# Pooled attention feeding a four-expert MoE: two-bank attention, a first batch pooled by matmuls, and fixed slots for batch 1

## The chip, the cores and the metric

The kernel runs on one core of a Trainium2 chip. The metric is device time in microseconds (us) of one execution. "Before" takes 545.05 us, the median of its first 3 runs (544.22 to 545.55).

Engines, as the profile names them: PE is the matmul engine, PEld its weight loads, DVE the vector engine, ACT the scalar engine, POOL the engine that issues the loads, SP the engine that issues the stores and DMA transposes. Times in the text are us from the start of the span unless something else is said. The span of a profile is about 2 us shorter than the device time of the same run.

## The reference

```python
# shortened: the softmax is written out in the reference, and out starts as zeros
def _attn_ref(q, k, v):                      # B=8, H=8, S=576, D=64
    k_p = k.reshape(B, H, S // 8, 8, D).mean(axis=3)      # pool 8 keys into 1: 72 keys
    v_p = v.reshape(B, H, S // 8, 8, D).mean(axis=3)
    scores = q @ k_p.transpose(0, 1, 3, 2) / sqrt(D)
    attn = softmax(scores)
    return attn @ v_p

def _moe_ref(x, domain_probs, w1, w2):       # x: 4608 x 512, E=4, F=1024
    p = domain_probs / (domain_probs.sum(-1, keepdims=True) + 1e-09)
    for e in range(E):
        out += p[:, e:e + 1] * (np.maximum(x @ w1[e], 0) @ w2[e])
```

Every token goes through all four experts, so nearly all the arithmetic is the MoE: two matmul layers, four times.

## The kernel before

The tokens are taken in nine chunks of 512 (eight batches, then the 8 x 64 left-over tokens). A *step* is one chunk through one expert. While PE works on the experts of chunk b, the attention of batch b+1 is done in small *pieces* between its matmuls.

The up-projection is a seven-product scheme (`up_seven`) in two halves j. Each half has four *slots*, `between(0)` to `between(3)`. In a slot PE does a share of the `down` matmuls of the step before, and the next attention piece is issued. DVE takes its instructions in the order issued (a trace below shows it). The code that the argument needs, with cuts marked:

```python
    def fold(raw, hs):                                    # DVE: 8 rows -> 4 -> 2
        nc.vector.tensor_add(out=raw[:, hs, 0:4, :], in0=raw[:, hs, 0:4, :], in1=raw[:, hs, 4:8, :])
        nc.vector.tensor_add(out=raw[:, hs, 0:2, :], in0=raw[:, hs, 0:2, :], in1=raw[:, hs, 2:4, :])

    def fold_keys(b, hs):                                 # 2 -> 1, written twice
        raw = raws[("kraw", b)]
        fold(raw, hs)
        for dup in range(2):
            nc.vector.tensor_add(out=kps[b % 2][0:SP, hs, dup, :], in0=raw[:, hs, 0, :], in1=raw[:, hs, 1, :])
    # ... fold_values: the same, written once
    # ... attention(b), for b >= 2, is a list of pieces, one popped whenever `due` reaches 1:
        add(opening)             # DMA transpose of q; fold_keys over all 8 heads; loads of b+1
        add(folded_values)       # fold_values over all 8 heads
        for _ in range(3):
            add(lambda: None)    # an empty piece: a pause
        for pair in range(NPAIR):
            add(lambda pair=pair: scores(b, pair))
            add(lambda pair=pair: exps(b, pair, 1))
    # ... then 4 x (context, context, turn), 3 pauses, combine_x

    def up_seven(c, e, j, between):
        # ...
        g, d, s = bank(), bank(), bank()                  # three PSUM banks
        product(c, e, j, 1, g, True)
        r1 = keep(g)                                      # ACT copies the bank to SBUF
        between(0)
        product(c, e, j, 2, s, True)
        relu_sum(top[:, :, 0:TH], s, r1)                  # DVE, relu-sum #1
        product(c, e, j, 6, g, False)
        r2 = keep(g)
        between(1)
        product(c, e, j, 5, d, True)
        product(c, e, j, 7, g, False)
        r3 = keep(g)
        relu_sum(low[:, :, TH:NT], d, r3)                 # DVE, relu-sum #2
        between(2)
        product(c, e, j, 4, g, False)
        nc.scalar.activation(out=low[:, :, 0:TH], in_=g[:], func=ACT.Relu)
        between(3)
        product(c, e, j, 3, d, False)
        relu_sum(top[:, :, TH:NT], d, r2)                 # DVE, relu-sum #3

    def down(c, e, j, n):                                 # slot n of half j
        first = (0, 3, 7, 12, 16)                         # 3, 4, 5, 4 matmuls
        for at in range(first[n], first[n + 1]):
            r, fc = 2 * j + at // FCH, at % FCH
            # ... one 128x512 matmul into sums[r]
            if fc == FCH - 1:                             # at = 7 and 15: slots 2 and 3
                merge(c, e, r, sums[r])                   # DVE; ACT for expert 0

    # ... the loads, in issue order:
        load_k(0); load_q(0); load_v(0); load_w1(0); load_probs(); load_w1(1)
        load_w2(0); load_w1(2); load_w2(1); load_w1(3)
        attention_first(); norm_probs(); combine_x(0)
        load_k(1); load_q(1); load_v(1); load_w2(2); load_w2(3)   # ...
```

Some words for what follows. A *fold* adds rows of k or v pairwise on DVE, until one row stands for eight. PSUM is the memory, in banks, into which PE writes its results. A *relu-sum* adds such a bank to the copy that ACT kept of another one, and sets negative values to 0. *Forms* are the sums and differences of weight blocks, or of blocks of x, that the seven products multiply.

The softmax here doesn't subtract the row's maximum and nothing guards it: scores larger than these inputs give would overflow.

Of the kernel before, what the change touches and what calls it, by code (L numbers as in the profile page):

```python
# [18 lines left out]
def kernel(  # L19
# [25 lines left out]
    SPP = 80  # L45
    BIG = 3.0e38
# [15 lines left out]
    psum_a = ctx.enter_context(tc.tile_pool(name="psum_a", bufs=3, space=bass.MemoryType.PSUM))  # L62
    psum_h = ctx.enter_context(tc.tile_pool(name="psum_h", bufs=3, space=bass.MemoryType.PSUM))
    psum_o = ctx.enter_context(tc.tile_pool(name="psum_o", bufs=2, space=bass.MemoryType.PSUM))
# [11 lines left out]
    def groups(b):  # L76

        n = 2 if b == 0 else 1
        return [slice(i * H // n, (i + 1) * H // n) for i in range(n)]

    def load_kv(b, src, nm):
        raw = rawpool.tile([SP, H, POOL, D], BF16, name=nm)
        for hs in groups(b):
            nc.gpsimd.dma_start(
                out=raw[:, hs], in_=src[b, hs].rearrange("h (j r) d -> j h r d", r=POOL)
            )
        raws[(nm, b)] = raw

    def load_q(b):
        q_sb = qpool.tile([P, H, NR, D], BF16, name="q_sb")  # L90
        for hs in groups(b):
            nc.gpsimd.dma_start(  # L92
                out=q_sb[:, hs].rearrange("p h r d -> p h (r d)"),
                in_=q[b, hs, 0:NT, :].rearrange("h (p r) d -> p h (r d)", r=NR),
            )
        raws[("q", b)] = q_sb

# [57 lines left out]

    def fold(raw, hs):
        nc.vector.tensor_add(out=raw[:, hs, 0:4, :], in0=raw[:, hs, 0:4, :],  # L157
                             in1=raw[:, hs, 4:8, :])
        nc.vector.tensor_add(out=raw[:, hs, 0:2, :], in0=raw[:, hs, 0:2, :],  # L159
                             in1=raw[:, hs, 2:4, :])  # L160

    def by_dma(b):
        return b >= 2
# [8 lines left out]
    def keys(b, hs):  # L172
        if hs.start == 0:
            state[("kpT", b)] = apool.tile([P, H, SPP], BF16, name="kpT", bufs=3)
        if by_dma(b):
            nc.sync.dma_start_transpose(
                out=state[("kpT", b)][:], in_=kps[b % 2][:].rearrange("j h u d -> j (h u d)")
            )
            return
        kpt_ps = psum_a.tile([P, H, SP], BF16, tag="a", name="kpt_ps")  # L180
        for h in range(hs.start, hs.stop):
            nc.tensor.transpose(kpt_ps[:, h, :], kps[b % 2][0:SP, h], ident[:SP, :SP])  # L182
        nc.vector.tensor_copy(out=state[("kpT", b)][:, hs, 0:SP], in_=kpt_ps[:, hs])
# [8 lines left out]
    def queries(b, pair):  # L192
        q_sb = raws[("q", b)]
        if pair == 0:
            state[("qT", b)] = apool.tile([P, H, 2, P], BF16, name="qT", bufs=1)
        if by_dma(b):
            nc.sync.dma_start_transpose(
                out=state[("qT", b)][:].rearrange("c h r p -> c (h r) p"),
                in_=q_sb[:].rearrange("p h r d -> p (h r d)"),
            )  # L200
            return
        pool, tag = (psum_o, "o_ps") if b == 0 else (psum_a, "a")
        qt_ps = pool.tile([P, 2, 2, P], BF16, tag=tag, name="qt_ps")
        for hh in range(2):
            for rr in range(2):
                nc.tensor.transpose(
                    qt_ps[:, hh, rr, :], q_sb[:, 2 * pair + hh, 2 * rr:2 * rr + 2, :], ident[:]
                )
        copy = nc.scalar.copy if b == 0 and pair % 2 else nc.vector.tensor_copy
        copy(out=state[("qT", b)][:, 2 * pair:2 * pair + 2], in_=qt_ps[:])  # L210

    def scores(b, pair):
        kpT, qT = state[("kpT", b)], state[("qT", b)]
        if pair == 0:
            state[("expT", b)] = apool.tile([SP, H, 2, 2, P], BF16, name="expT", bufs=1)
        both = [psum_a.tile([P, 2, 2, P], F32, tag="a", name="sc_ps") for _ in range(2)]
        for hh in range(2):
            h = 2 * pair + hh
            for r2 in range(2):
                lo = r2 * D  # L220
                nc.tensor.matmul(  # L221
                    both[r2][0:SP, hh], lhsT=kpT[lo:lo + D, h, 0:SP], rhs=qT[lo:lo + D, h]
                )
        state[("sc", b, pair)] = both
        exps(b, pair, 0)

    def exps(b, pair, r2):
        nc.scalar.activation(  # L228
            out=state[("expT", b)][:, 2 * pair:2 * pair + 2, :, r2, :],
            in_=state[("sc", b, pair)][r2][0:SP], func=ACT.Exp, scale=EXP_SCALE,  # L230
        )

    def divide(c_ps, x_tok, half):
        inv = npool.tile([P, NPAIR], F32, name="inv")
# [6 lines left out]
    def context(b, r, half):  # L241
        expT, vp = state[("expT", b)], vps[b % 3]
        if ("x", b, r) not in state:
            state[("x", b, r)] = npool.tile([P, 2, NPAIR, D], BF16, name="x_tok", bufs=5)
        pool, tag = (psum_h, "h_ps") if b == 0 and half else (psum_a, "a")
        c_ps = pool.tile([P, NPAIR, D + 1], F32, tag=tag, name="c_ps")
        for i in range(NPAIR):
            h = half * NPAIR + i
            nc.tensor.matmul(  # L249
                c_ps[:, i, :], lhsT=expT[:, h, r // 2, r % 2, :], rhs=vp[:, h, :]  # L250
            )
        divide(c_ps, state[("x", b, r)], half)

    def flip(x_tok, dst, on_dma, copy=nc.vector.tensor_copy):
        flat = x_tok[:].rearrange("p a h d -> p (a h d)")
        if on_dma:
            nc.sync.dma_start_transpose(out=dst, in_=flat)
            return
        xt_ps = psum_a.tile([P, NPAIR, P], BF16, tag="a", name="xt_ps")
        for kc in range(KC):  # L260
            nc.tensor.transpose(xt_ps[:, kc, :], flat[:, kc * P:(kc + 1) * P], ident[:])  # L261
        copy(out=dst, in_=xt_ps[:])

    def turn(b, r):
        if r == 0:
            state[("xT", b)] = xpool.tile([P, KC, NT], BF16, name="xT")
        flip(state.pop(("x", b, r)), state[("xT", b)][:, :, r * P:(r + 1) * P], by_dma(b),
             nc.scalar.copy if b == 0 else nc.vector.tensor_copy)

    def rem_queries(i):  # L270
        q_rem = q_rems.pop(i)
        qTr = apool.tile([P, NPAIR, 2, REM], BF16, name="qTr")
# [6 lines left out]
    def rem_scores(i):  # L279
        qTr = state.pop(("qTr", i))  # L280
        both = [psum_a.tile([P, 2, NPAIR, REM], F32, tag="a", name="scr_ps") for _ in range(2)]
        for bb in range(2):
            kpT = state[("kpT", 2 * i + bb)]
            for pair in range(NPAIR):
                for hh in range(2):
                    lo = hh * D
                    nc.tensor.matmul(
                        both[hh][0:SP, bb, pair, :], lhsT=kpT[lo:lo + D, 2 * pair + hh, 0:SP],
                        rhs=qTr[lo:lo + D, pair, bb, :],
                    )  # L290
        expTr = apool.tile([SP, 2, 2, NPAIR, REM], BF16, name="expTr")
        for hh in range(2):
            nc.scalar.activation(out=expTr[:, hh], in_=both[hh][0:SP],
                                 func=ACT.Exp, scale=EXP_SCALE)
        state[("expTr", i)] = expTr

    def rem_context(i):
        expTr = state.pop(("expTr", i))
        x_tok = npool.tile([P, 2, NPAIR, D], BF16, name="x_tok", bufs=5)
        for half in range(2):  # L300
            c_ps = psum_a.tile([P, NPAIR, D + 1], F32, tag="a", name="c_ps")
            for j in range(NPAIR):
                h = half * NPAIR + j
                for bb in range(2):
                    nc.tensor.matmul(
                        c_ps[bb * REM:(bb + 1) * REM, j, :],
                        lhsT=expTr[:, h % 2, bb, h // 2, :], rhs=vps[(2 * i + bb) % 3][:, h, :],
                    )
            divide(c_ps, x_tok, half)
        state[("xr", i)] = x_tok  # L310

    def rem_turn(i):
        flip(state.pop(("xr", i)), x_rem[:, :, i * P:(i + 1) * P], True)

    def attention_first():

        lo, hi = groups(0)
        fold_keys(0, lo)
        keys(0, lo)
        fold_keys(0, hi)  # L320
        keys(0, hi)
        for pair in range(NPAIR):
            queries(0, pair)
            if pair:
                scores(0, pair - 1)
                exps(0, pair - 1, 1)
        scores(0, NPAIR - 1)
        exps(0, NPAIR - 1, 1)
        for half, hs in enumerate((lo, hi)):
            fold_values(0, hs)  # L330
            for r in range(NR):
                context(0, r, half)
                if half and r:
                    turn(0, r - 1)
        turn(0, NR - 1)

    def attention(b):

        every = slice(0, H)
# [4 lines left out]
        def opening():  # L344
            if by_dma(b):
                queries(b, 0)
            fold_keys(b, every)
            if by_dma(b):
                keys(b, every)
                load_next()  # L350

        def load_next():
# [5 lines left out]
        def folded_values():  # L358
            fold_values(b, every)
# [3 lines left out]
        def queried(pair):  # L363
            queries(b, pair)
            if pair == NPAIR - 1:
                load_next()

        add(opening)
        add(folded_values)
        if by_dma(b):  # L370
            for _ in range(3):
                add(lambda: None)
        else:
            add(lambda: keys(b, every))
            add(lambda: queried(0))
        for pair in range(NPAIR):
            if not by_dma(b) and pair + 1 < NPAIR:
                add(lambda pair=pair: queried(pair + 1))
            add(lambda pair=pair: scores(b, pair))
            add(lambda pair=pair: exps(b, pair, 1))  # L380
        for r in range(NR):
            add(lambda r=r: context(b, r, 0))
# [254 lines left out]
```

## Time and profile before

| reading | before |
|---|---|
| device time | 545.05 us |
| span of the profile | 543.2 us |
| first expert's first matmul | 25.22 |
| first expert done | 33.85 |
| PE's wait for the folded keys of batch 1 | 3.68 us, up to 54.30 |
| batch 1's first expert starts | 87.43 |
| PE's waits on relu-sums after that | 4.1 us, 6 times |

(87.43 is the fifth matmul of a row of eight in PE's timeline: its start, 87.00, and four steps of 0.109 us.)

From the page of before: the busy line (busy us, share of the span, instructions), then rows that cut the span into 40 slices of 13.6 us. The digits are tenths of a slice; the last row is GB/s moved.

```profile
PE 511.9 (94%) x3736; PEld 328.7 (61%) x3736; DVE 322.4 (59%) x599; ACT 233.5 (43%) x403; POOL 45.7 (8%) x64
...
PE   2696999999999999999999999999999999999996
...
GB/s 122 197 206 200 196 109 1 136 133 31 93 152 38 19 21 111 153 28 70 121 90 23 28 51 165 65 69 32 59 17 25 35 53 1 11 40 39 2 1 77
```

PE is short of full in slices 1, 2 and 4, all before 55 us, and in the last one. In slices 2 and 4 the loads run at about 200 GB/s. From slice 5 to the last but one PE's row is 9s, which leaves two things to gain: the start, and any single waits that a slice of 13.6 us does not show. A word of caution on the 94%: the Trainium skill ("Trainium Kernel Development and Optimization", section "Best Practices") says not to judge the distance to the roofline by matmul busy time. This trace agrees: records of 128x256 matmuls are 273 ns long, but four of them take 0.60 us, so they start 0.109 us apart and the records overlap.

The waits view of before, of PE alone (what was waited for: us in total, times, longest us):

```profile
PE kpt_ps L182 <- DVE kp L169: 14.4, 3, 7.8
PE g_ps L432 <- DVE H_sb L470: 4.1, 6, 0.8
PE c_ps L249 <- DVE vp L188: 2.5, 1, 2.5
```

The first line is the wait for folded keys: 7.8 and 2.9 us of it in the first attention, 3.68 in batch 1's. The second is the wait on relu-sums.

The windows view of before (start:end, length, busy us and count of PE, PEld, DVE, ACT, POOL, then the granted PE clock, the DMA share and GB/s):

```profile
50.00:60.00 10.00, 5.97 (x32) 3.32 (x30) 6.26 (x10) 0.97 (x2) 0.54 (x1) 0.66 1.30 201
...
88.00:540.00 452.00, 445.40 (x3261) 287.63 (x3258) 268.59 (x479) 199.04 (x344) 16.27 (x20) 1.00 0.32 59
```

After the wait at 50.6 to 54.3 the clock is down to 0.66 for those ten microseconds; in the long stretch after 88 it is full.

The timeline of before, PE's rows (start, us, engine, line, operation, count, and in brackets the idle time before it and what ended it):

```profile
25.22 8.79 PE L450 MATMUL h_ps<-xT,w_bf 128*128 128x512 bf16 x32 [0.67 <-ACT xT L262]
33.85 0.60 PE L432 MATMUL g_ps<-xT,w_bf 128*128 128x256 bf16 x4
...
54.30 0.66 PE L182 MATMUL kpt_ps<-ident,kp 72*128 72x72 bf16 x8 [3.68 <-DVE kp L169]
...
106.27 1.03 PE L432 MATMUL g_ps<-xf,w_bf 128*128 128x256 bf16 x8 [0.81 <-DVE H_sb L470]
```

And DVE's rows around that last wait:

```profile
98.67 1.21 DVE L157 TENSOR_TENSOR kraw<-kraw 72x2048 bf16<-72x2048 bf16 x1
...
101.31 0.68 DVE L470 CUSTOM_DVE_ANT_0 H_sb<-g_ps,r 128x512 bf16<-128x512 f32 x1
101.91 0.74 DVE L515 SCALAR_TENSOR_TENSOR acc<-o_ps,p_all,acc 128x512 f32<-128x512 f32 x1
102.57 1.21 DVE L157 TENSOR_TENSOR vraw<-vraw 72x2048 bf16<-72x2048 bf16 x1
...
104.88 0.74 DVE L515 SCALAR_TENSOR_TENSOR acc<-o_ps,p_all,acc 128x512 f32<-128x512 f32 x1
105.54 1.27 DVE L470 CUSTOM_DVE_ANT_0 H_sb<-g_ps,r 128x512 bf16<-128x512 f32 x2
```

The whole key fold (98.67 to 101.31) stands in slot 1, ahead of relu-sum #2. The whole value fold stands in slot 2. Relu-sum #3 comes at 105.54, and PE waits for it 0.81 us, because the next half's product 5 goes into the bank that it reads. The batch after this one waits once too (0.55 us).

### The profile page before, as it was taken

Reading aid. Unit: us, or ns where it says so; the run is one execution under the profiler, and the core shown is the slowest. Engines: PE = TensorE matmul, PEld = TensorE weight load, DVE = VectorE, ACT = ScalarE, POOL = GpSimd, SP = SyncE. Lnnn points to the kernel's source line nnn. Section 1 sums busy time; section 2 is a strip of 40 time slices with the busy share of each in tenths; the row PEclk is TensorE's granted clock in tenths of the full one; section 3 lists DMA queues with packets and bytes.
Section 4 is the critical chain, followed back from the end, with each engine's and each line's share of the span. In section 5 each row is a group of like instructions: output and inputs, shape, how many; then the busy total and the mean of one; then the engine's idle time right before and its main releaser. Section 6 shows DMA issues by size and latency. Waiting matters only on the chain.

```text
span 543.2 us, 9149 instructions
## 1 busy us (share of the span) xinstructions
PE 511.9 (94%) x3736; PEld 328.7 (61%) x3736; DVE 322.4 (59%) x599; ACT 233.5 (43%) x403; POOL 45.7 (8%) x64
## 2 busy tenths in 40 slices
PE   2696999999999999999999999999999999999996
PEld 1354556566656666566666665666566666666663
DVE  3725588837773767367836665568456644554453
ACT  1463343473346333643373345533653345334430
POOL 6632100200110000201100002000000000000000
PEclk9999899999999999999999999999999999999999
DMA  8999980681781014914831119331101010011003
GB/s 122 197 206 200 196 109 1 136 133 31 93 152 38 19 21 111 153 28 70 121 90 23 28 51 165 65 69 32 59 17 25 35 53 1 11 40 39 2 1 77
DMA packets 72954, 40.98 MB, mean 75 GB/s; under 512 B 42688, under 2 KB 68288, under 8 KB 72912
## 3 DMA queue, kind: packets, MB, share of 16 engines
q0 software_dynamic: 33744, 22.63, 29.2%
q1 hardware_dynamic: 39168, 17.77, 14.0%
q8 instruction: 29, 0.48, 0.4%
q14 instruction: 13, 0.11, 0.1%
HBM read 45.16 MB, written 9.44 MB: 101 GB/s over the span
## 4 chain that ended last, share of the span: by engine, by line
PE 84%; DVE 9%; DMA 5%; issue 1%; ACT 0%; POOL 0%; POOLq 0%; DVEq 0%
PE o_ps L501 41%; PE g_ps L432 36%; DMA vraw<-in_v_dram 4%; PE sc_ps L221 2%; DVE H_sb L470 2%; DVE acc L515 2%; PE h_ps L450 2%; PE c_ps L249 1%; DMA kraw<-in_k_dram 1%; DVE vraw L157 1%; DVE kraw L157 1%; DVE vraw L159 1%; PE xt_ps L261 1%; DVE kp L169 1%; DVE x_tok L236 0%
## 5 line engine op out<-in xcount | busy, mean ns | idle before, releaser
L501 PE MATMUL o_ps<-w_bf,H_sb 128*128 128x512 bf16 x1152 | 295.6, 380 | 0.0
L470 DVE CUSTOM_DVE_ANT_0 H_sb<-g_ps,r 128x512 bf16<-128x512 f32 x210 | 143.8, 687 | 162.6 <-ACT r L466 90.3
L432 PEld LDWEIGHTS <-w_bf 128*128 128x128 bf16 x1960 | 185.3, 98 | 75.7 <-issue 11.7
L466 ACT COPY r<-g_ps 128x512 f32<-128x512 f32 x210 | 123.1, 586 | 208.4 <-PE g_ps L432 206.7
L432 PE MATMUL g_ps<-xf,w_bf 128*128 128x256 bf16 x1120 | 157.6, 274 | 6.4 <-DVE H_sb L470 4.1
L501 PEld LDWEIGHTS <-H_sb 128*128 128x128 bf16 x1152 | 113.0, 98 | 76.6 <-issue 0.8
L432 PE MATMUL g_ps<-xT,w_bf 128*128 128x256 bf16 x744 | 101.8, 273 | 0.0
L515 DVE SCALAR_TENSOR_TENSOR acc<-o_ps,p_all,acc 128x512 f32<-128x512 f32 x108 | 80.5, 746 | 21.1 <-PE o_ps L501 21.1
L487 ACT ACTIVATE H_sb<-g_ps 128x512 bf16<-128x512 f32 x70 | 41.8, 598 | 48.2 <-PE g_ps L432 48.2
L228 ACT ACTIVATE expT<-sc_ps 72x512 bf16<-72x512 f32 x64 | 37.1, 592 | 12.5 <-PE sc_ps L221 12.3
L236 DVE TENSOR_TENSOR x_tok<-c_ps,inv 128x256 bf16<-128x256 f32 x72 | 30.6, 425 | 2.5
L92 POOL DMA_DIRECT2D q_sb<-in_q_dram x9 | 7.9, 876 | 237.1 <-DMA qT<-q_sb 230.2
L512 ACT ACTIVATE acc<-o_ps,p_all 128x512 f32<-128x512 f32 x36 | 24.9, 691 | 4.7 <-PE o_ps L501 4.7
L249 PEld LDWEIGHTS <-expT 72*128 72x128 bf16 x256 | 16.2, 102 | 15.3 <-issue 3.1
L235 DVE RECIPROCAL inv<-c_ps 128x4 f32<-128x4 f32 x72 | 12.7, 177 | 14.6 <-PE c_ps L249 11.9
L249 PE MATMUL c_ps<-vp,expT 72*128 72x65 bf16 x256 | 18.4, 200 | 2.8 <-DVE vp L188 2.5
L221 PE MATMUL sc_ps<-qT,kpT 64*72 64x256 bf16 x128 | 14.5, 298 | 1.4 <-DVE qT L210 0.9
L182 PE MATMUL kpt_ps<-ident,kp 72*128 72x72 bf16 x16 | 1.5, 251 | 14.4 <-DVE kp L169 14.4
L221 PEld LDWEIGHTS <-kpT 64*72 64x72 bf16 x128 | 5.4, 111 | 13.8 <-issue 12.9
L157 DVE TENSOR_TENSOR kraw<-kraw 72x2048 bf16<-72x2048 bf16 (+1 forms) x9 | 9.9, 1096 | 5.8 <-DMA kraw<-in_k_dram 5.8
L432 PE MATMUL g_ps<-x_rem,w_bf 128*128 128x256 bf16 x96 | 13.3, 273 | 0.0
L157 DVE TENSOR_TENSOR vraw<-vraw 72x2048 bf16<-72x2048 bf16 (+1 forms) x9 | 9.9, 1095 | 3.7 <-DMA vraw<-in_v_dram 3.7
(54 smaller groups left out, 140.9 us busy)
## 6 DMA issues: line engine op xcount, KB each, us to landing
out_dram<-acc SPq DMA_DIRECT2D x32, 256.0 KB, 2.5
w_bf<-in_moe_w_dram POOLq DMA_DIRECT2D x16, 256.0 KB, 11.3
w_bf<-in_moe_w_dram POOLq DMA_DIRECT2D x4, 1024.0 KB, 18.3
kraw<-in_k_dram POOLq DMA_DIRECT2D x7, 576.0 KB, 10.3
vraw<-in_v_dram POOLq DMA_DIRECT2D x7, 576.0 KB, 11.8
q_sb<-in_q_dram POOLq DMA_DIRECT2D x7, 512.0 KB, 6.9
out_dram<-acc SPq DMA_DIRECT2D x8, 128.0 KB, 2.3
kraw<-in_k_dram POOLq DMA_DIRECT2D x2, 288.0 KB, 5.8
```

The lines of the kernel that those rows point to most:

```text
L157: nc.vector.tensor_add(out=raw[:, hs, 0:4, :], in0=raw[:, hs, 0:4, :], in1=raw[:, hs, 4:8, :])
L221: nc.tensor.matmul(both[r2][0:SP, hh], lhsT=kpT[lo:lo + D, h, 0:SP], rhs=qT[lo:lo + D, h])
L228: nc.scalar.activation(out=state[("expT", b)][:, 2 * pair:2 * pair + 2, :, r2, :], in_=state[("sc", b, pair)][r2][0:SP], func=ACT.Exp, sca ...
L236: nc.vector.tensor_tensor(out=x_tok[:, half], in0=c_ps[:, :, 0:D], in1=inv[:].unsqueeze(2).to_broadcast([P, NPAIR, D]), op=ALU.mult,)
L249: nc.tensor.matmul(c_ps[:, i, :], lhsT=expT[:, h, r // 2, r % 2, :], rhs=vp[:, h, :])
L432: nc.tensor.matmul(bank[:, t, :], lhsT=w1_bf[:, e, block, kc, lo:lo + P], rhs=x[:, kc, :], start=(first and t == 0 and kc == 0), stop=(t = ...
L466: nc.scalar.copy(out=r[:], in_=ps[:])
L470: nc.vector._custom_dve(TENSOR_ADD_SAT, out=out, in0=ps[:], in1=r[:], s0=BIG, s1=0.0)
L487: nc.scalar.activation(out=low[:, :, 0:TH], in_=g[:], func=ACT.Relu)
L501: nc.tensor.matmul(sums[r][:], lhsT=hidden[(c, e)][:, fc, r * P:(r + 1) * P], rhs=w2_bf[:, e, fc, :], start=(fc == 0), stop=(fc == FCH - 1),)
L512: nc.scalar.activation(out=accs[(c, r)][:], in_=o_ps[:], func=ACT.Copy, scale=prob)
L515: nc.vector.scalar_tensor_tensor(out=dst, in0=o_ps[:], scalar=prob, in1=dst, op0=ALU.mult, op1=ALU.add,)
```

## The change

Its intent is a shorter start and less work for DVE and ACT:

1. **First attention.** Pooling of k and v of batch 0 by matmuls with a 0/1 matrix in place of DVE adds; k and v over 96 partitions instead of 72; dummy matmuls (`warm`) to bring PE's clock up; loads in the order k, q, v.
2. **First expert by token halves**, so it can start when two of four token blocks are turned. The second expert becomes plain, because its weight forms are no longer made.
3. **Batch 1's attention in fixed slots 19 to 31** rather than evenly from slot 16 on.
4. **Later batches.** A pair's scores go to a two-bank PSUM tile, so one exp of 72x1024 stands for two of 72x512, and one divide of 128x512 for two of 128x256. Folds go in head halves.

Two smaller edits come along: the PSUM bank that is left over goes to the `down` sums (`psum_o`, three instead of two), and the weight forms are made one per slot instead of four in a block after a step.

```diff
+    FR = 96
+    FT = S // FR
 ...
-    psum_a = ctx.enter_context(tc.tile_pool(name="psum_a", bufs=3, space=bass.MemoryType.PSUM))
+    psum_a = ctx.enter_context(tc.tile_pool(name="psum_a", bufs=1, space=bass.MemoryType.PSUM))
 ...
+    def two_banks():
+        return psum_a.tile([P, 2, NT], F32, tag="a", name="two")
 ...  (scores: both halves of a pair into one two-bank tile, one exp)
+        two = two_banks()
         nc.scalar.activation(
-            out=state[("expT", b)][:, 2 * pair:2 * pair + 2, :, r2, :],
-            in_=state[("sc", b, pair)][r2][0:SP], func=ACT.Exp, scale=EXP_SCALE,
-        )
+            out=state[("expT", b)][:, 2 * pair:2 * pair + 2].rearrange("j h r s p -> j s (h r) p"),
+            in_=two[0:SP].rearrange("j s (a p) -> j s a p", p=P),
+            func=ACT.Exp, scale=EXP_SCALE,
+        )
 ...  (first batch: pooling by matmul)
+                    nc.tensor.matmul(
+                        kpt_ps[hh * D:(hh + 1) * D, i * SP:(i + 1) * SP],
+                        lhsT=raws["k"][:, 2 * pair + hh, r, :], rhs=pool_map[:, r, :],
+                        start=(r == 0), stop=(r == FT - 1),
+                    )
 ...  (batch 1: a table of slots)
+            19: [lambda: fold_keys(1, lo), lambda: fold_keys(1, hi)],
+            20: [second_keys],
+            21: [lambda: second_queries(0)],
+            22: [lambda: second_queries(1)],
+            23: [lambda: scores(1, 0)],
+            24: [lambda: scores(1, 1), lambda: fold_values(1, lo)],
+            25: [lambda: scores(1, 2), lambda: fold_values(1, hi)],
+            26: [lambda: scores(1, 3)],
+            27: [lambda: context(1, 0), lambda: turn(1, 0)],
 ...
+            30: [lambda: context(1, 3), lambda: turn(1, 3)],
+            31: [loads, lambda: load_v(2), lambda: combine_x(1)],
 ...  (batches 2 to 7: the pieces)
-        add(opening)
-        add(folded_values)
-        if by_dma(b):
-            for _ in range(3):
-                add(lambda: None)
+        add(lambda: (queries(b), fold_keys(b, lo)))
+        add(keyed)                          # fold_keys(b, hi), DMA transpose, loads
+        add(lambda: fold_values(b, lo))
+        add(folded_values)                  # fold_values(b, hi), load
+        rest(2)                             # two pauses
         for pair in range(NPAIR):
             add(lambda pair=pair: scores(b, pair))
-            add(lambda pair=pair: exps(b, pair, 1))
+            rest()
         for r in range(NR):
-            add(lambda r=r: context(b, r, 0))
-            add(lambda r=r: context(b, r, 1))
+            add(lambda r=r: context(b, r))
+            add(lambda r=r: turn(b, r))
+        rest(3)
+        add(lambda: combine_x(b))
 ...  (the loads)
         load_w1(0)
+        load_w2(0)
+        attention_first()
         load_probs()
         load_w1(1)
-        load_w2(0)
         load_w1(2)
         load_w2(1)
         load_w1(3)
-        attention_first()
         load_k(1)
```

## The prediction

> **What bounds the kernel now.** By the busy table PE is busy 511.9 of 543.2 us (94%); in the chain of waits PE holds 84%. From 87 us on PE bounds it: a seven-product expert takes 6.51 us per token half, and PE waits only 4.9 us in all (waits view: 4.1 us on the DVE's relu-sum, just where a whole 72x2048 fold sits on DVE). The rest of the loss is before 87 us. Timeline: the first expert starts at 25.2 us with matmuls 0.43 us apart (half clock) for 3.4 us and ends at 34.0; experts 1 to 3 and batch 1's attention last until 87.4. There PE waits 3.7 us for the folded keys of batch 1 (50.6 to 54.3), then runs at a clock of 0.66 (windows view, 50 to 60 us). That wait is DMA: about 200 GB/s move from 13 to 68 us, k of batch 1 lands at 51.5, v at 56.75.
>
> **What the change does.**
> 1. First attention: fold adds (1.4 to 1.6 us of DVE per half, k and v) become matmuls with a pooling matrix; dummy matmuls keep PE warm. k and v are spread over 96 partitions instead of 72: the Trainium skill ("DMA: Bandwidth & Descriptors", section "Why a DMA increments its semaphore by 16 and not by 1") says that the partition count decides how many of 16 engines carry a transfer. The trace agrees loosely: 0.59 MB of k took 3.8 us where 0.26 MB weight blocks took 1.25. Estimate: q, v and w1 of expert 0 land 2 us sooner. Exps then run from about 11.3 to 15.9 instead of 13.1 to 17.9; divides of 0.65 us on DVE follow; token halves let the first expert start after two of four turns. Estimate: start at 19.3, warm, end at 26.8 against 34.0. Gain 7.2 us.
> 2. Expert 1 becomes plain: 32x0.216 instead of 56x0.109 us. Loss 0.9 us.
> 3. Slots 19 to 31: keys of batch 1 are still bound by DMA (landing estimated at 48.5 to 49.5). PE reaches them at about 47.4 and DVE needs 3.3 us of folds, so a stall of 3 to 5 us remains, with a cold clock after it ("TensorE: Matmul & The Clock Gate", Part 1; the 0.66 clock agrees). Expert 3 then carries about 18 us of DVE work in 15.5 us of PE work, and ends in DMA transposes (2.4 us) before combine_x. Of the 6.3 us some 1.5 are given back here; the weight-form waits (0.6, 1.0, 0.8 us) go away.
> 4. Steady state: folds in halves, one exp of 72x1024 (about 1.0 us for two of 0.59), one divide of 512. DVE and ACT time there is off the path; only the 4.1 us of relu-sum waits can go. Single-buffered two-bank scores and long exps may cost 1 us. Net gain 2.5 us.
>
> Sum: 7.2 - 0.9 - 1.5 + 2.2 + 2.5 = about 9.5 us.
>
> **Predicted time: 535.5 us, range 529 to 542.** Chances: faster by over 2% (below 534.1 us) 0.40, within 2% 0.58, slower 0.02.
>
> **What would show it.** Timeline: first expert's matmuls start near 19.3 us, 0.11 us apart; expert 1 ends near 40.7; a PE wait on the second kpt of 3 to 5 us near 48 to 52; batch 1's first expert near 80 instead of 87.4. Waits view: PE's waits on the relu-sum after 90 us fall from 4.1 to under 1.5 us.
>
> **What would make it wrong.** k of batch 1 landing before 47 (no stall, near 531); DVE overload in slots 20 to 31 or late w2 blocks costing over 4 us (near 540); long exps delaying the keep copies in every batch (near 542).

## More of the kernel before

A *merge* adds a finished `down` sum, weighted with the expert's probability, to the output.

Pieces are popped at len(pieces)/30 per slot: 35 or 29 pieces over 30 slots before, 32 or 26 after. So every piece stands in a somewhat different slot than before, whatever it does.

Between relu-sum #2 and relu-sum #3 lie two slots, 2 and 3, and both merges. Between any other two relu-sums lies one slot and no merge.

## The result, and the profile after

After: **539.99 us** (539.07 to 540.56), against 545.05 before. The ratio is 0.9896, 95% interval 0.9861 to 0.993: within 2%. (A ratio here is the mean time of one kernel's runs over that of the other's of the same rounds, so not quite the ratio of the medians that are quoted.) The prediction was 535.5 with a range of 529 to 542 and "within 2%" as the likeliest class. Range and class hold, but of the 9.5 us of gain only about 5.1 came (spans: 543.2 − 538.1; 5.7 by the ratio).

The same lines of the page, after:

```profile
PE 516.0 (96%) x3811; PEld 330.2 (61%) x3811; DVE 310.0 (58%) x560; ACT 230.5 (43%) x371; POOL 46.8 (9%) x66
...
PE   8896998899999999999999998999999999999996
...
GB/s 136 203 204 201 193 125 68 158 65 72 77 155 10 41 12 129 133 30 94 113 68 31 20 66 173 45 68 52 40 12 29 49 42 1 10 40 40 2 0 79
```

PE's first two slices are now 8s (part of that is the dummy matmuls), but slice 4 still is a 6, and DMA runs at the same 200 GB/s as before. Slices 7 and 8 (81 to 108 us) have become 8s; waits of PE that are read below stand there. DVE lost 12.4 us of busy time and ACT 3.0.

PE's waits after:

```profile
PE g_ps L569 <- DVE H_sb L622: 6.0, 9, 0.8
PE kpt_ps L272 <- DVE kp L190: 4.8, 2, 3.7
PE g_ps L569 <- DVE xf L558: 1.8, 1, 1.8
```

The relu-sum waits, which were to fall to under 1.5 us, rose to 6.0 us in 9 waits.

Windows after; the stretches are set to this kernel's own landmarks:

```profile
48.00:60.00 12.00, 7.16 (x45) 4.19 (x43) 7.08 (x16) 2.40 (x4) 0.00 (x0) 0.72 1.29 203
...
80.00:535.00 455.00, 445.70 (x3261) 287.75 (x3258) 266.66 (x466) 196.24 (x316) 16.24 (x20) 1.00 0.31 59
```

The long stretch holds the same 3261 matmuls with the same busy time as before (445.4 and 445.7 us), so what differs there is waits. (The lengths of the two stretches are only where I cut them.) To see by how much, take a wait that recurs every two batches: before, from the wait that ended at 155.39 to the one at 267.93, 112.54 us; after, from 149.11 to 262.41, 113.30 us.

PE's timeline, after:

```profile
18.84 1.91 PE L600 MATMUL h_ps<-xT,w_bf 128*128 128x256 bf16 x16 [0.41 <-ACT xT L385]
...
26.49 0.81 PE L653 MATMUL o_ps<-w_bf,H_sb 128*128 128x512 bf16 x3
...
52.49 0.42 PE L272 MATMUL kpt_ps<-ident,kp 72*128 72x72 bf16 x4 [3.68 <-DVE kp L190]
54.07 0.42 PE L272 MATMUL kpt_ps<-ident,kp 72*128 72x72 bf16 x4 [1.16 <-DVE kp L190]
...
99.22 1.03 PE L569 MATMUL g_ps<-xf,w_bf 128*128 128x256 bf16 x8 [0.84 <-DVE H_sb L622]
```

The start is as predicted: 18.84 (19.3 predicted), warm (16 matmuls in 1.91 us), done at 26.49 (26.8 predicted).

And DVE, just before the wait that ends at 99.22:

```profile
93.39 0.69 DVE L622 CUSTOM_DVE_ANT_0 H_sb<-g_ps,r 128x512 bf16<-128x512 f32 x1 [1.79 <-ACT r L618]
94.00 0.74 DVE L667 SCALAR_TENSOR_TENSOR acc<-o_ps,p_all,acc 128x512 f32<-128x512 f32 x1
94.66 0.68 DVE L181 TENSOR_TENSOR kraw<-kraw 72x1024 bf16<-72x1024 bf16 x1
...
96.24 0.74 DVE L667 SCALAR_TENSOR_TENSOR acc<-o_ps,p_all,acc 128x512 f32<-128x512 f32 x1
96.90 0.68 DVE L181 TENSOR_TENSOR kraw<-kraw 72x1024 bf16<-72x1024 bf16 x1
...
98.48 0.68 DVE L622 CUSTOM_DVE_ANT_0 H_sb<-g_ps,r 128x512 bf16<-128x512 f32 x1
99.08 0.68 DVE L181 TENSOR_TENSOR vraw<-vraw 72x1024 bf16<-72x1024 bf16 x1
```

Relu-sum #2, merge, half fold, merge, half fold, relu-sum #3. PE had finished the product that relu-sum #3 reads by about 96.0; the relu-sum starts at 98.48. It stood in the queue. The Trainium skill ("Perfetto Trace Analysis", section "Tensor Engine Instruction (MATMUL, LD_WEIGHTS)") says that ACT and DVE are strict FIFO, and this agrees: work that nobody needs yet goes first, because it was issued first. The delay then carries on: the value halves stand in the next two slots, and PE waits once more, 0.54 us at 103.17.

Where the 5.1 us come from, by landmarks:

| landmark | before | predicted | after |
|---|---|---|---|
| first expert's first matmul | 25.22 | 19.3 | 18.84 |
| first expert done | 33.85 | 26.8 | 26.49 |
| third expert starts | 46.87 | 40.7 | 40.30 |
| keys of batch 1 landed (first fold starts) | 51.51 | 48.5 to 49.5 | 50.76 |
| PE's wait for those keys | 3.68 us | 3 to 5 us | 4.84 us |
| batch 1's first expert | 87.43 | about 80 | 79.45 |
| lead at about 92 us (the same matmul group at 85.08 and 92.11) | | 7.0 | 7.03 |
| relu-sum waits after that | 4.1 us, 6 times | under 1.5 us | 6.0 us, 9 times |
| lead at the end | | 9.5 | 5.1 |

Lead at 92 us was 7.03, as the first terms of the prediction's sum give (7.2 − 0.9 − 1.5 + 2.2 = 7.0). That it fits so closely is luck. In five profiles whose code is the same up to there (after, e1, e2, e11, e12; the experiments are below) the first score matmul of the left-over tokens starts at 87.6, 87.5, 85.8, 89.1 and 89.5, against 94.6 in the one profile of before: a lead of 5.1 to 8.8 us. Between 92 us and the end the lead shrank by 1.9 instead of growing by 2.5.

**One trap in reading these waits.** The page counts PE's idle time from the end of its records, and the skill's same section says that those ends are estimated. Here a 128x512 record is 379 ns long at a cadence of 216 ns, so each wait that follows such a matmul is shown 0.163 us too short. By this count nine waits of 6.0 us in all cost 6.0 + 9 × 0.163 = 7.5 us; the experiments test it.

### The profile page after: what moved, and what is told of

The parts are those of the page before. It is cut to its first block, busy times and chain, and to the rows that moved or that the text cites. A ratio compares the mean times of both kernels' runs of the same rounds, so it can differ in the third digit from the quotient of the medians. Undisturbed runs are those within 1.5% of the kernel's fastest.

```text
span 538.1 us, 9237 instructions
## 1 busy us (share of the span) xinstructions
PE 516.0 (96%) x3811; PEld 330.2 (61%) x3811; DVE 310.0 (58%) x560; ACT 230.5 (43%) x371; POOL 46.8 (9%) x66
## 4 chain that ended last, share of the span: by engine, by line
PE 78%; DVE 10%; DMA 8%; POOL 1%; ACT 1%; issue 1%; DVEq 0%; POOLq 0%
PE o_ps L653 39%; PE g_ps L569 36%; DMA w_bf<-in_moe_w_dram 4%; DMA kraw<-in_k_dram 3%; DVE H_sb L622 2%; DVE acc L667 2%; PE two L225 2%; PE two L348 1%; DVE kraw L181 1%; DVE kp L190 1%; ACT r L618 1%; DVE kraw L183 1%; DVE vraw L181 1%; POOL w_bf L134 1%; DVE vraw L183 0%
## 5 line engine op out<-in xcount | busy, mean ns | idle before, releaser
L622 DVE CUSTOM_DVE_ANT_0 H_sb<-g_ps,r 128x512 bf16<-128x512 f32 x204 | 139.7, 688 | 155.8 <-ACT r L618 88.4
L569 PE MATMUL g_ps<-xf,w_bf 128*128 128x256 bf16 x1088 | 152.7, 273 | 6.2 <-DVE H_sb L622 4.4
L229 ACT ACTIVATE expT<-two 72x1024 bf16<-72x1024 f32 x28 | 28.5, 1018 | 10.7 <-PE two L225 10.7
L330 DVE TENSOR_TENSOR x_tok<-two,inv 128x512 bf16<-128x512 f32 x32 | 22.1, 692 | 1.1
L329 DVE RECIPROCAL inv<-two 128x8 f32<-128x8 f32 x32 | 6.5, 204 | 14.2 <-PE two L348 11.0
L348 PE MATMUL two<-vp,expT 72*128 72x65 bf16 x224 | 11.9, 194 | 0.5 <-DVE x_tok L330 0.5
L134 POOL DMA_DIRECT2D w_bf<-in_moe_w_dram x16 | 11.5, 726 | 9.3 <-DMA w_bf<-in_moe_w_dram 9.2
L225 PE MATMUL two<-qT,kpT 64*72 64x256 bf16 x112 | 11.5, 283 | 0.4 <-DVE qT L286 0.4
L181 DVE TENSOR_TENSOR kraw<-kraw 72x1024 bf16<-72x1024 bf16 x14 | 9.5, 678 | 2.0 <-DMA kraw<-in_k_dram 2.0
L181 DVE TENSOR_TENSOR vraw<-vraw 72x1024 bf16<-72x1024 bf16 x14 | 9.5, 678 | 0.0
## 6 DMA issues: line engine op xcount, KB each, us to landing
w_bf<-in_moe_w_dram POOLq DMA_DIRECT2D x4, 1024.0 KB, 16.8
```

The costliest lines, as they stand in the source:

```text
L225: nc.tensor.matmul(two[0:SP, r2].rearrange("j (h r p) -> j h r p", h=2, r=2)[:, hh], lhsT=kpT[lo:lo + D, h, 0:SP], rhs=qT[lo:lo + D, h],)
L229: nc.scalar.activation(out=state[("expT", b)][:, 2 * pair:2 * pair + 2].rearrange("j h r s p -> j s (h r) p"), in_=two[0:SP].rearrange("j ...
L330: nc.vector.tensor_tensor(out=x_tok[:], in0=c_ps[:, :, :, 0:D], in1=inv[:].unsqueeze(3).to_broadcast([P, 2, NPAIR, D]), op=ALU.mult,)
L348: nc.tensor.matmul(bank[:, i * (D + 1):(i + 1) * (D + 1)], lhsT=expT[:, h, r // 2, r % 2, :], rhs=vp[:, h, :],)
L569: nc.tensor.matmul(bank[:, t, :], lhsT=w1_bf[:, e, block, kc, lo:lo + P], rhs=x[:, kc, :], start=(first and t == 0 and kc == 0), stop=(t = ...
L622: nc.vector._custom_dve(TENSOR_ADD_SAT, out=out, in0=ps[:], in1=r[:], s0=BIG, s1=0.0)
```

## The experiments

**Theory A (slots).** The loss after 92 us is a matter of position: the four half folds stand in adjacent slots, two of them in slots 2 and 3, where the merges are. **Rival B (wider operations).** The two-bank scores with one buffer, the exp of 72x1024 and the divide of 128x512 hold PE or DVE up. **Theory C (DMA).** The start is bound by the load stream, so what is won ahead of the keys of batch 1 is lost in the wait for them. **Rival D.** The start is limited by PE and DVE and every microsecond saved ahead of the keys reaches the end.

Twelve kernels ran, all correct. All are the kernel after with the edit shown or described. Each ran timed against the kernel before, in four groups on four occasions, whose medians for before were 545.11, 545.18, 544.98 and 545.91 us.

| run | edit | median us | ratio to before, 95% |
|---|---|---|---|
| e1_spread | half folds apart | 531.97 | 0.9747 (0.9716 to 0.9778) |
| e2_whole | folds whole | 546.88 | 1.0013 (0.998 to 1.0046) |
| e5_whole_phase | whole, in the slots of before | 536.42 | 0.9843 (0.9826 to 0.986) |
| e12_slots01 | half folds adjacent, slots 0 and 1 | 533.0 | 0.9756 (0.9729 to 0.9784) |
| e4_fr72 | 72 partitions | 542.0 | 0.9929 (0.9898 to 0.9959) |
| e6_no_warm | no dummy matmuls | 540.75 | 0.992 (0.9907 to 0.9934) |
| e10_no_halves | first expert whole | 539.24 | 0.9891 (0.9862 to 0.992) |
| e3_k_early | k of batch 1 sooner | 538.14 | 0.9858 (0.9831 to 0.9884) |
| e7_spread_k_forms | e1 + e3 + forms moved | 530.66 | 0.9734 (0.972 to 0.9748) |
| e8_plus | e7 + two small moves | 529.55 | 0.9718 (0.9704 to 0.9731) |
| e9_w2_first | e8 + w2 before v | 530.73 | 0.9722 (0.9694 to 0.975) |
| e11_after_again | none (control) | 539.68 | 0.9894 (0.9867 to 0.9921) |

### Position of the folds: e1, e2, e5, e12

**e1_spread** keeps every operation and moves the half folds apart. The score, context and turn pieces keep their slots, so only folds move, with the key transpose and the loads that go with them:

```diff
         add(lambda: (queries(b), fold_keys(b, lo)))
-        add(keyed)
-        add(lambda: fold_values(b, lo))
-        add(folded_values)
-        rest(2)
+        rest()
+        add(keyed)
+        rest(3)
         for pair in range(NPAIR):
             add(lambda pair=pair: scores(b, pair))
-            rest()
+            if pair == 0:
+                add(lambda: fold_values(b, lo))
+            elif pair == 1:
+                add(folded_values)
+            else:
+                rest()
```

> The changed kernel with the half folds of batches 2 to 7 taken out of four adjacent slots (a free slot between the key halves, the value halves after the first two score pieces). Theory A (adjacent half folds plus merges overfill the DVE, and its relu-sum comes late): PE's waits on the relu-sum after 85 us fall from 6.0 us to under 1.5, time about 4 to 5 us under the changed kernel, near 535.5. Rival B (the long exp of 72x1024 or the single two-bank buffer delays PE): waits stay near 6 us, time near 540.

Measured: 531.97 us, and PE's waits view has no line for relu-sums at all. Span 530.6, 7.5 us less than after: the 7.5 us that nine waits cost by the corrected count. DVE in e1:

```profile
96.18 0.74 DVE L671 SCALAR_TENSOR_TENSOR acc<-o_ps,p_all,acc 128x512 f32<-128x512 f32 x1
96.84 0.68 DVE L626 CUSTOM_DVE_ANT_0 H_sb<-g_ps,r 128x512 bf16<-128x512 f32 x1
97.44 0.68 DVE L181 TENSOR_TENSOR kraw<-kraw 72x1024 bf16<-72x1024 bf16 x1
```

The second merge is now followed at once by the relu-sum, and the second half fold comes after it. The wide exps and divides are all still there, so rival B can't explain the 7.5 us.

**e2_whole** goes the other way: folds over all heads in one piece each, key fold and value fold in adjacent pieces.

```diff
-        add(lambda: (queries(b), fold_keys(b, lo)))
-        add(keyed)
-        add(lambda: fold_values(b, lo))
-        add(folded_values)
-        rest(2)
+        add(lambda: (queries(b), keyed()))     # keyed: fold_keys(b, every)
+        add(folded_values)                     # fold_values(b, every)
+        rest(4)
```

> The changed kernel with the folds of batches 2 to 7 whole again, keys in one slot and values in the next, as the kernel before has them. Theory A: six waits on the relu-sum with about 4.1 us as before, so about 2 us under the changed kernel, near 538. Rival B: nine or ten waits with 6 us as in the changed kernel, near 540.

My expectation missed by 9 us: 546.88, as slow as before. I had taken it that whole folds would wait as they did before. They don't stand where they stood before. Here they fell into slots 2 and 3, one behind each merge. PE's waits view and timeline of e2:

```profile
PE g_ps L567 <- DVE H_sb L620: 10.0, 6, 2.6
```

```profile
99.28 1.03 PE L567 MATMUL g_ps<-xf,w_bf 128*128 128x256 bf16 x8 [2.63 <-DVE H_sb L620]
```

The miss is worth more than a hit. It says that size is not what decides; but it left open whether the folds' slots did it or something else of after. So:

**e5_whole_phase** is e2 with three more pauses at the end of the list, so that there are as many pieces per batch as before and the whole folds fall into the slots that they had before:

```diff
             add(lambda r=r: turn(b, r))
-        rest(3)
+        rest(6)
```

> The whole folds of e2_whole, with three more empty pieces at the end of each batch, so that folds fall into the slots that they have in the kernel before (about one slot earlier than in the changed kernel). If the relu-sum waits come from where the folds fall (adjacent pieces, and which slot of the expert): six waits of about 4.1 us in all as in the kernel before, in place of 10.0 us in e2_whole, so about 6 us under e2_whole, near 539. If they come from the wider exp and divide: waits stay near 10 us, time near 546.

Measured: 536.42, and

```profile
PE g_ps L567 <- DVE H_sb L620: 3.9, 6, 0.7
```

as expected, like the 4.1 us in 6 waits of before. Three pauses at the end of a list, which do nothing themselves, are worth 9 to 10 us between e2 and e5. The waits shown differ by 6.1 us only; the check over the whole stage below says where the rest went. With the folds in the slots of before, the kernel with two-bank scores, wide exps and wide divides has the waits of before: rival B falls.

**e12_slots01** asks whether it is adjacency or the slot. The four half folds stay in two adjacent pairs, but in slots 0 and 1 of a half, where no merge is:

```diff
+        base = SLOTS * (b - 1)
+        placed.update({
+            base + 8: [lambda: (queries(b), fold_keys(b, lo))],
+            base + 9: [keyed],
+            base + 12: [lambda: fold_values(b, lo)],
+            base + 13: [folded_values],
+        })
```

(The four pieces leave the list, pauses take their place, and the pauses behind `scores` go.)

> The changed kernel with the half folds of batches 2 to 7 still in adjacent slots, two and two, but always in the first two slots of an expert's half, each of which is followed by a relu-sum and has no merge (the last two slots hold both merges and only one relu-sum after both). If the slot decides, and not the spacing alone: waits on the relu-sum near 0, time near that of e1_spread, about 8 us under the changed kernel, near 532. If adjacency itself makes the wait: 4 us of waits or more remain, near 538.

Measured: 533.0 us, no relu-sum wait after 86 us. (Its profiled run had a start about 2 us longer than that of after: 6.0 us of waits for the keys.) DVE in e12:

```profile
97.15 0.75 DVE L669 SCALAR_TENSOR_TENSOR acc<-o_ps,p_all,acc 128x512 f32<-128x512 f32 x1 [0.41 <-PE o_ps L655]
97.82 0.68 DVE L624 CUSTOM_DVE_ANT_0 H_sb<-g_ps,r 128x512 bf16<-128x512 f32 x1
98.42 0.68 DVE L181 TENSOR_TENSOR kraw<-kraw 72x1024 bf16<-72x1024 bf16 x1
...
99.99 0.68 DVE L624 CUSTOM_DVE_ANT_0 H_sb<-g_ps,r 128x512 bf16<-128x512 f32 x1
100.59 0.68 DVE L181 TENSOR_TENSOR kraw<-kraw 72x1024 bf16<-72x1024 bf16 x1
```

A relu-sum goes after each half fold. Adjacent is fine; slots 2 and 3 together are not.

**The waits add up.** Take the time from the first merge's start, right after relu-sum #2, to relu-sum #3's start, from the timelines around the first fold that waits. Relu-sum #2 itself starts 2.44 us before PE's next group of three `down` matmuls in after and e1, 2.43 in e2, but 1.61 in before (101.31 against 102.92), so there it was already 0.83 late, behind the whole key fold.

| kernel | merge to relu-sum #3 | relu-sum #2 late by | sum | PE's wait | sum less wait |
|---|---|---|---|---|---|
| e1 | 96.84 − 93.95 = 2.89 | 0 | 2.89 | 0 | |
| before | 105.54 − 101.91 = 3.63 | 0.83 | 4.46 | 0.81 | 3.65 |
| after | 98.48 − 94.00 = 4.48 | 0 | 4.48 | 0.84 | 3.64 |
| e2 | 98.55 − 92.27 = 6.28 | 0 | 6.28 | 2.63 | 3.65 |
| e5 | 99.03 − 95.40 = 3.63 | 0.77 | 4.40 | 0.74 | 3.66 |

The last column is the slack of relu-sum #3 at this place: 3.65 us in four kernels, with waits as the view shows them, so about 3.5 by the corrected count. Up to that DVE may do anything there for free; beyond it, PE waits microsecond for microsecond. Two merges take 1.3 us of it (0.66 each from start to start), and a half key fold 1.58 (94.66 to 96.24). One half fold fits (2.89), two don't (4.48).

**The same over the whole stage.** The scores of the left-over tokens are computed four times (`qTr` is their q), the first time near 90 us and the last near 450. The tile view of before, after, e1 and e2 gives the first and last start of these matmuls:

```profile
L287 PE MATMUL scr_ps<-qTr,kpT x64: 196/196/217, 94.6 to 455.3; 64*72 64x64 bf16 x64
L405 PE MATMUL two<-qTr,kpT x64: 196/196/217, 87.6 to 450.5; 64*72 64x64 bf16 x64
L405 PE MATMUL two<-qTr,kpT x64: 196/196/217, 87.5 to 443.0; 64*72 64x64 bf16 x64
L405 PE MATMUL two<-qTr,kpT x64: 196/196/217, 85.8 to 455.6; 64*72 64x64 bf16 x64
```

| kernel | first to last | relu-sum waits, corrected | rest |
|---|---|---|---|
| before | 360.7 | 5.1 | 355.6 |
| after | 362.9 | 7.5 | 355.4 |
| e1 | 355.5 | 0 | 355.5 |
| e12 | 355.5 | 0 | 355.5 |
| e5 | 360.3 | 4.9 | 355.4 |
| e2 | 369.8 | 11.0 | 358.8 |

Five kernels agree within 0.2 us once the waits are taken off. So the places of the folds explain the whole difference in this stage, and the wide operations, which before doesn't have, cost nothing and bring nothing there. Only e2 has 3.3 us more. The clock explains it: behind two of its three waits of 2.6 us, at 213.75 and 329.88, the granted clock was 0.72 over 6 us, and five 128x512 matmuls took 2.34 us (214.97) where e5 has 1.24. In after and before the clock is 1.00 throughout this stage.

### The start: e4, e6, e10, e3

**e4_fr72** puts k and v of batch 0 back over 72 partitions, eight rows each instead of six:

```diff
-    FR = 96
+    FR = 72
```

> The changed kernel with the first k and v on 72 partitions of 8 rows instead of 96 of 6. If the DMA stream as a whole is the limit[...]: k and v of batch 0 land 1 to 2 us later each, but w1 of expert 0 still ends near 20.1 us and k of batch 1 near 50.7; first expert starts up to 1 us later, time within 0.5 us of the changed kernel. The prediction's rival (partitions set the rate of the stream): everything behind v lands about 2 us later, k of batch 1 near 52.5, time about 2 us more.

Measured: 542.0, about 2 us over after: in time what the rival said; the landings lie between the two theories. The values of batch 0 landed at 14.8 and 16.8 instead of 12.7 and 14.1, and the first expert's w1 at 21.4 instead of 20.1, but k of batch 1 was issued only 1.3 us later. So, in one profile of each, 96 partitions are worth 2 us and more for the transfer itself and about 1.3 for those behind it. That other transfers fill a part of what a narrow one leaves idle would fit, but no view here shows it. The profiled run was its slowest (544.05) and had a cold clock at the start, with the third expert 7 us later than after, of which 3 us had gone by batch 1's first expert. It is a poor witness for more than the landings.

**e6_no_warm** leaves the dummy matmuls out (`warm` returns at once).

> The changed kernel without its dummy matmuls. If they are worth what the prediction gave them: the first expert's matmuls run at half clock for some 3 us as before, first expert ends 1.5 to 3 us later than 26.5, but k of batch 1 still lands near 50.7 and its keys hold PE until about 54, so that only part reaches the end: time 0.5 to 2 us over the changed kernel. If they do nothing: no change.

Measured: 540.75. In the profile the first expert started at 21.10 (18.84 after), cold (16 matmuls in 3.49 us), and the third at 44.15 (40.30): 3.85 us lost. At the end 0.8 us are left (spans 538.9 and 538.1). PE's waits in e6:

```profile
PE kpt_ps L272 <- DVE kp L190: 2.9, 2, 1.6
```

The wait for keys was 4.8 us and is 2.9: PE was 3.85 us later at the third expert, the first fold of the keys only 1.0 us later (51.79 against 50.76). This is what theory C says.

**e10_no_halves** takes the token halves out of the first expert, so that it starts after all four turns (and after `norm_probs` and `combine_x(0)`, which move ahead of it).

> The changed kernel with the first expert over all 512 tokens again, after all four turns. Expected: first expert starts near 21.5 instead of 18.84 and ends 1.5 to 2.5 us later than 26.5; as k of batch 1 still lands near 50.7, most of that is taken back at the wait on its keys, so time 0 to 1 us over the changed kernel. If the start is worth its full size: 2 us over.

Measured: 539.24, the same as after within the intervals (and as the control, 539.68). The third expert started 2.4 us later, and the wait for keys shrank to 2.9. The token halves give nothing at the end.

**e3_k_early** issues the load of k of batch 1 before w1 of expert 3:

```diff
-        load_w1(3)
         load_k(1)
+        load_w1(3)
         load_q(1)
```

> The changed kernel with k of batch 1 loaded ahead of w1 of expert 3. If the stall at the second keys is DMA's: k lands near 46 instead of 50.7, the PE waits on kp fall from 4.8 us to 2 to 3 us (3.3 us of folds remain), the first expert of batch 1 starts about 2 us earlier unless the forms of expert 3 (landing 3 us later) now wait; time 537 to 539. If the folds alone make the stall: waits on kp unchanged, time near 540.

Measured: 538.14, 1.9 us less than after. The keys had landed by 45.3, but their folds began at 49.19, behind weight forms in DVE's queue; PE's wait fell from 4.8 to 2.9 only. The profiled run's first expert was half cold again, though nothing in that stretch differs from after: 16 matmuls in 3.52 us. In the profiles of after, e1, e2, e7, e8, e9, e11 and e12 they took 1.91; in e3, e4, e5 and e6 3.44 to 3.57. The skill ("TensorE: Matmul & The Clock Gate", Part 1) says that the clock opens after a busy window of about 3.4 us that runs freely, so that the same kernel warms up at different points from run to run. e3 and e5, which differ from after in nothing ahead of that point, agree. So a single profile can't show a gain or loss of 1.6 us there.

### Building on it: e7, e8, e9

**e7_spread_k_forms** is e1 and e3 together, with the forms of expert 0's weights moved out of the way of batch 1's key folds:

```diff
-                forms_due.extend(nothing + combine_w1(2))
+                forms_due.extend(combine_w1(0) + combine_w1(2))
             elif s == 2:
-                forms_due.extend(combine_w1(0) + combine_w1(3))
+                forms_due.extend(nothing + combine_w1(3))
```

> e1_spread and e3_k_early together, and the weight forms of expert 0 made in slots 8 to 11, where the DVE idles 7.9 us, instead of 16 to 19. Theory: the parts add up. Relu-sum waits after 85 us near 0 (6.0 us plus nine matmul latencies of 0.16 us in the changed kernel), waits on kp 1.5 to 2.5 us instead of 4.8: time 3 us under e1_spread, near 529. If the start is bound elsewhere (late w1 of expert 3 or the forms): near 532.

Measured: 530.66. Folds began at 46.97 and the wait for keys fell to 2.2 us; but the ratio is only 0.0013 under e1's, some 0.7 us. Where it went, in PE's timeline of e7:

```profile
60.89 0.81 PE L657 MATMUL o_ps<-w_bf,H_sb 128*128 128x512 bf16 x3 [2.22 <-DMA w_bf<-in_moe_w_dram]
```

PE now arrives early at expert 2's down weights, which come through the same stream, and waits 2.2 us there (then 10 us at a clock of 0.83).

**e8_plus** is e7 with batch 1's key folds in slots 18 and 19 instead of both in 19, and its last token block turned on PE (`turn_here(1, 3)` in slot 31) instead of by DMA.

> e7_spread_k_forms, with the first half of batch 1's keys folded a slot earlier (slot 18), and the last 128 tokens of batch 1 turned by PE and ACT instead of by a DMA transpose. Expected: waits on kp 1 us less than in e7, wait of PE on the forms of x (1.8 us in the changed kernel) under 0.8 us: time 1.5 to 2 us under e7, near 527.5. Should the DVE wait for k in slot 18 (landing near 45.3), the gain is smaller.

Measured: 529.55 (529.08 to 530.25), the fastest of all: 2.8% faster than before and 10 us faster than after. Key wait 1.8 us, w2 wait 2.4.

**e9_w2_first** is e8 with the load of w2 of expert 2 issued before v of batch 1, the value folds one slot later.

> e8_plus, with w2 of expert 2 loaded ahead of v of batch 1, and the values folded a slot later (25 and 26). If the DMA stream now holds the start (PE waited 2.4 us for w2 of expert 2 in e8): that wait goes, w2 lands near 58 instead of 60.7, the first expert of batch 1 starts about 2 us earlier, time near 527.5. If v of batch 1 now comes too late for slot 25: the wait moves to the DVE and the context, time near 529.5.

Measured: 530.73, no faster. PE's waits in e9:

```profile
PE g_ps L574 <- DMA xT<-x_tok: 2.3, 1, 2.3
PE kpt_ps L272 <- DVE kp L190: 1.8, 1, 1.8
...
PE two L348 <- DVE vp L202: 1.1, 1, 1.1
PE o_ps L658 <- DMA w_bf<-in_moe_w_dram: 0.8, 1, 0.8
```

The w2 wait shrank from 2.4 to 0.8, a wait for values (1.1) came, and one for the transposed tokens grew from 0.8 to 2.3. Reordering moves the wait about; these four sum to 6.0 us, against 5.0 in e8. The stream delivers about 200 GB/s from 13 to 68 us whatever the order (200 in after and e3, 202 in e8, 201 in e9). Together with e6 and e10, rival D falls.

**e11_after_again** is after unchanged, as a control:

> The changed kernel once more, unaltered, as the control for these runs: ratio to the kernel before near 0.990, 540 us.

Measured: 539.68, ratio 0.9894 (0.9896 the first time), relu-sum waits again 6.0 us in 9.

## Why the prediction was right or wrong

The measured time lies in the range, but that is no proof of the sum: its first terms fit, partly by luck, and its last had the wrong sign.

- **Step 1, first attention, 7.2 us: right.** First expert done 7.36 us sooner (33.85 − 26.49). This profile of after had warm first matmuls; e3 and e5, with the same code there, took 1.5 to 1.6 us longer over them.
- **Step 2, plain expert, −0.9: right.** Third expert 6.57 us sooner: 0.8 lost.
- **Step 3, keys bound by DMA: mechanism right, one input off.** The estimate "q, v and w1 of expert 0 land 2 us sooner" became "landing estimated at 48.5 to 49.5" for k of batch 1; it was 50.76, 0.75 us sooner than before and not 2 to 3. Both kernels move the same bytes ahead of k at 200 GB/s, and by e4 the wider spread of the early transfers is worth about 1.3 us there. One profile is weak evidence: with the same code ahead of it, the first fold of these keys began between 49.24 (e2) and 52.31 (e12). The wait was at the top of the 3 to 5 us predicted (4.84). The feared DVE overload in expert 3 cost a wait of 1.8 us on the forms of x and little else. The sum over steps 1 to 3, 7.0, was 7.03, which is luck as far as the hundredths go: the keys came later than estimated, the feared overload cost less, and the start differs by 3.7 us from profile to profile.
- **Step 4 failed: "Net gain 2.5 us" was −1.9.** The words were "only the 4.1 us of relu-sum waits can go". I saw "a whole 72x2048 fold sits on DVE" at each wait and inferred that folds of half the size would not be waited for. The runs showed that the slot counts, and how much of DVE's queue stands ahead of relu-sum #3: about 3.5 us are free (3.65 by the waits as shown). The change puts two half folds and two merges there, 4.48 us, and the waits rose to 6.0. Shown by e1 (same operations, elsewhere: waits gone, 7.5 us), e2 (whole folds in those slots: 10.0 us), e5 (whole folds in the slots of before: 3.9) and e12 (adjacent, other slots: none).
- **The named danger, "long exps delaying the keep copies in every batch", did not come.** e1 has all the long exps and no such wait.
- **What the two-bank tiles bought:** 12.4 us of DVE and 3.0 us of ACT busy time, first attention included. No run here shows a gain from it, and the check over the whole stage shows none: 355.4 to 355.6 us with and without them, waits taken off. Both engines are off the critical path after 92 us, except where DVE's *order* puts them on it. Fewer pieces per batch did have an effect, by moving the folds.
- **Not in the prediction:** gains ahead of the key wait were partly worthless already. e6 and e10 lose 3.85 and 2.4 us by the third expert, and 0.8 to 1.3 (medians, ratios) and 0 at the end. So of step 1, the dummies and the halves bought an early start and little time; the 96 partitions bought about 2 us (e4). How the rest of the lead divides between pooling by matmuls, the slots of batch 1 and the missing waits for weight forms, no run separates.

## What to carry to other kernels

Filler work on an in-order engine should be placed by the slack of the next instruction behind it that somebody waits for, not by its size and not by the engine's busy share; after any change in the number of filler pieces, look up in which slots they now fall. Time won ahead of a wait that DMA bounds was handed back here in that wait, wholly (e10) or for the most part (e6), so first ask what the load stream would still deliver late. Counting a wait's shown time plus the overhang of modelled matmul records made the account of the long stage close within 0.2 us in five kernels. Before trusting a lead read from one profile, look how far the same code scatters: here by 3.7 us.

## What the Trainium skill lacked or had wrong

- "DMA: Bandwidth & Descriptors", section "Why a DMA increments its semaphore by 16 and not by 1": the partition count decides how many engines carry one transfer, but nothing there says what that is worth when more transfers are queued behind. Here 96 instead of 72 partitions brought the values of batch 0 in by 2.1 to 2.7 us sooner, and the issue of the load of k of batch 1, far behind in the same queue, by 1.3 us only (e4 against after, one profile each).
- "Perfetto Trace Analysis", section "Tensor Engine Instruction (MATMUL, LD_WEIGHTS)": it says that matmul ends are estimated, but not that idle time counted from them comes out too short. Here each PE wait that follows a 128x512 matmul is 0.163 us longer than shown (record 379 ns, cadence 216), and nine waits of 6.0 us in all cost 7.5 us of span (after against e1).
- The same page says that DVE is strict FIFO; no page that I read says what follows for filler work, that the slack ahead of a waited-for instruction is a number to be read off: 3.65 us here by the waits as shown, in four kernels.
- "TensorE: Matmul & The Clock Gate", Part 1: agrees. One more instance of its run-to-run warm-up: the same first attention left the first expert's first 16 matmuls at 1.91 us (after, e1, e11) or 3.52 us (e3).
